# The opening of a fused attention and feed-forward kernel: half of k by a hardware queue, q in token quarters, v in three pieces

## The chip, the cores and the metric

The kernel runs on one core of a Trainium2 chip. A core has a matrix engine (TensorE, PE in the profile), a vector engine (VectorE, DVE), a scalar engine (ScalarE, ACT), a general engine (GpSimd, POOL), a queue engine for transfers (SyncE, SP) and 16 DMA engines that move data between HBM and the on-chip memory SBUF. Matrix products land in PSUM banks and must be copied out by DVE or ACT. Each engine works through its own instructions strictly in program order; they meet at semaphores. The metric is the device time of one execution in microseconds (us).

## The reference

```
k_proj = einsum('ks,bhsd->bhkd', E, k)      # E: [64, 1024]
v_proj = einsum('ks,bhsd->bhkd', F, v)
attn   = softmax(q @ k_proj^T / sqrt(64))   # over 64 projected keys
o      = attn @ v_proj                      # 8 batches, 8 heads, 1024 tokens, 64
x      = o, heads side by side              # [8192 tokens, 512]
g      = x @ w_gate                         # [512, 1536]
out    = (g * sigmoid(g) * (x @ w_val)) @ w_out
```

Everything comes in as float32 and is worked on in bfloat16 with float32 sums.

## The kernel before

**Tiling.** A batch is cut into two chunks of 512 tokens (`ch`); the feed-forward layer works chunk by chunk (`c` = 2 x batch + `ch`), each chunk in 12 tiles of 128 hidden columns (`f`). For each `f` there are four gate products into a bank of kind "g" and four value products into a bank of kind "v" (`f_mm`, L314, 512 columns each), a tanh on ACT (L334), two vector instructions on DVE (L341, L346), and later the products with `w_out` (L360). There are two "g" banks, so the gate products of `f` = 2 wait until DVE has read the gate of `f` = 0.

**Attention units.** `u_KV` (L137) projects k or v for a range of heads: eight accumulating products over the tokens, then for k one ACT copy (`ks`, L157), for v two ACT copies in batch 0 into the block-diagonal `BDV` (L162, L163). `u_KT` (L167) transposes the projected k on PE and copies it into `BD` by four DVE copies (L180, L181). A chunk's queries are handled in four units `u`: `g` is the half of the heads and `i` the half of the chunk's tokens (units 0 and 1 are heads 0 to 3, units 2 and 3 heads 4 to 7; units 0 and 2 are the first token half, 1 and 3 the second). For each unit: `u_T` four transposes and one copy to `qT`; `u_S` four score products and the exponential on ACT (`ee`, L231); `u_R` sum and reciprocal on DVE; `u_N` the normalising multiply (L258; POOL for units 0 and 1, DVE for units 2 and 3 of batch 0); `u_A` four transposes and one copy to `AT`. `u_PV2` (L294) multiplies two head pairs of one token half by `BDV`, and its copy gives half a chunk of `xT` (two of four pairs), the input of `f_mm`.

**The order is written out by hand.** After the opening (L427 to L521), a slot table runs the feed-forward of chunk `c` with the attention of later batches laid between. The opening runs batch 0's first chunk's attention as its data land. All loads of q, k, v and weights are issued by POOL, which casts float32 to bfloat16 on the way, in this order: k heads 0 to 3, k heads 4 to 7, q heads 0 to 3, q heads 4 to 7, v heads 0 to 3, v heads 4 to 7, then the weights of `f` = 0, 1, 2-3, 4-5, then q of the second chunk, and the rest. SP loads E and F as they are. Loads on POOL and the `u_N` multiplies of POOL share one order. `warm(n)` is n products of zeros that keep PE busy. `turn(0)` and `turn(1)` transpose E and F.

**The end of the opening** is: `u_KV` of v heads 4 to 7, `u_PV2` twice for the first token half, `u_A(0,1)` and `u_A(0,3)`, gate and value of `f` = 0 on the first token half, `u_PV2` twice for the second half, then `f` = 1 on the first half. The loop begins with `f` = 0 and 1 on the second half and then takes whole chunks from `f` = 2.

Of the kernel before, what the change touches and what calls it, by code (L numbers as in the profile page):

```python
# [12 lines left out]
BF16 = mybir.dt.bfloat16  # L13
FP32 = mybir.dt.float32

B = 8
H = 8
S = 1024
D = 64
KP = 64  # L20
DM = H * D
DFF = 1536
P = 128
NJ = S // P
# [4 lines left out]
CW = 512  # L29
# [5 lines left out]
def kernel(  # L35
# [19 lines left out]
    nc = tc.nc  # L55
# [4 lines left out]
    kv_pool = ctx.enter_context(tc.tile_pool(name="kv", bufs=2))  # L60
# [22 lines left out]
    kb, vb, qb, xT, hT = {}, {}, {}, {}, {}  # L83

    def load_k(b, h0=0, h1=H):
        if h0 == 0:
            kb[b] = kv_pool.tile([P, H, NJ, D], BF16, name="kb", tag="kb")
        nc.gpsimd.dma_start(  # L88
            out=kb[b][:, h0:h1].rearrange("p h j d -> p h (j d)"),
            in_=k[b, h0:h1].rearrange("h (p j) d -> p h (j d)", j=NJ),  # L90
        )

    def load_v(b, heads=(0, H)):
        t = kv_pool.tile([P, H, NJ, D], BF16, name="vb", tag="vb")
        vb[b] = t
        for h0, h1 in zip(heads, heads[1:]):
            nc.gpsimd.dma_start(
                out=t[:, h0:h1].rearrange("p h j d -> p h (j d)"),
                in_=v[b, h0:h1].rearrange("h (p j) d -> p h (j d)", j=NJ),
            )  # L100

    def load_q(b, ch, parts=1):
        t = q_pool.tile([P, H, 4, D], BF16, name="qb", tag="qb")
        qb[b, ch] = t
        n = H // parts
        for i in range(parts):
            nc.gpsimd.dma_start(  # L107
                out=t[:, i * n : (i + 1) * n].rearrange("p h j d -> p h (j d)"),
                in_=q[b, i * n : (i + 1) * n].rearrange("h (p c j) d -> p c h (j d)", c=2, j=4)[:, ch],
            )  # L110

    def load_w_gv(c0, c1, which=(0, 1)):
        cs = slice(c0 * P, c1 * P)
        for wsrc, wdst in [((moe_w_gate, wg), (moe_w_val, wv))[i] for i in which]:
            nc.gpsimd.dma_start(
                out=wdst[:, :, cs],
                in_=wsrc[:, cs].rearrange("(t p) c -> p t c", p=P),
            )
# [11 lines left out]
    def bank(where, shape, dt, name):  # L130
        pool, tag = banks[where]
        return pool.tile(shape, dt, name=name, tag=tag)

    def copy(eng, out, in_):
        (nc.scalar.copy if eng is nc.scalar else eng.tensor_copy)(out=out, in_=in_)  # L135
# [51 lines left out]
    def u_T(b, u, at="a", eng=nc.scalar):  # L187
        ch, w = divmod(u, 4)
        g, i = divmod(w, 2)
        ps = bank(at, [P, 4, P], BF16, "qTp")  # L190
        src = qb[b, ch]
        for n in range(4):
            nc.tensor.transpose(  # L193
                out=ps[:, n, :],
                in_=src[:, 4 * g + n, 2 * i : 2 * i + 2, :].rearrange("p j d -> p (j d)"),
                identity=ident_bf[:],
            )
        t = aw.tile([P, 4, P], BF16, name="qT", tag="qT", bufs=4)
        copy(eng, t[:], ps[:])
        qT[b, u] = t  # L200
# [38 lines left out]
    def u_R(b, u):  # L239
        e = ee[b, u]  # L240
        z = aw.tile([P, 4, 2], FP32, name="zz", tag="zz", bufs=3)
        nc.vector.reduce_sum(out=z[:], in_=e[:], axis=AX.X)  # L242
        r = aw.tile([P, 4, 2], FP32, name="rr", tag="rr", bufs=4)
        nc.vector.reciprocal(out=r[:], in_=z[:])  # L244
        rr[b, u] = r
# [48 lines left out]
    def u_PV2(b, ch, g, i, eng):  # L294
# [11 lines left out]
            )  # L306
        copy(eng, xT[b, ch][:, 2 * g : 2 * g + 2, 256 * i : 256 * (i + 1)], ps[:])


    gp = {}  # L310

# [112 lines left out]
            fn(*a)  # L424

    with tc.manual_schedule():
        load_k(0, 0, 4)  # L427
        ef = []
        for which, src in (("E", E), ("F", F)):
            raw = const.tile([KP, S], FP32, name=f"{which}raw")  # L430
            nc.sync.dma_start(out=raw[:], in_=src)
            ef.append(raw)
        zeros = const.tile([P, CW], BF16, name="zeros")
        nc.vector.memset(zeros[:], 0.0)
        make_identity(nc, ident_fp[:])
        make_identity(nc, ident_bf[:])
        for i in range(2):
            nc.vector.memset(BD[i][:], 0.0)
            nc.vector.memset(BDV[i][:], 0.0)

        def turn(which):
            for half in range(2):
                ps = bank("v", [P, 4, KP], FP32, "efp")
                for i in range(4):
                    j = 4 * half + i
                    nc.tensor.transpose(
                        out=ps[:, i, :],
                        in_=ef[which][:, bass.ds(j, P, step=NJ)],
                        identity=ident_fp[:KP, :KP],
                    )  # L450
                js = slice(4 * half, 4 * half + 4)
                copy((nc.scalar, nc.vector)[which], (ET, FT)[which][:, js, :], ps[:])

        def warm(n):

            ps = bank("v", [P, CW], FP32, "warm")
            for _ in range(n):
                nc.tensor.matmul(
                    out=ps[:], lhsT=zeros[:, 0:P], rhs=zeros[:],
                    start=True, stop=True,  # L460
                )


        load_k(0, 4, 8)
        load_q(0, 0, 2)
        load_v(0, (0, 4, 8))
        load_w_gv(0, 1)
        load_w_gv(1, 2)
        load_w_gv(2, 4)
        warm(8)  # L470
        turn(0)
        turn(1)
        warm(7)
        u_KV(0, "k", (0, 4), at="y")
        warm(2)
        u_KT(0, at="v", prs=(0, 2))
        warm(2)
        u_KV(0, "k", (4, 8), at="y")
        warm(2)
        u_KT(0, at="v", prs=(2, 4))  # L480
        u_T(0, 0, "a", nc.scalar)
        u_T(0, 1, "a", nc.vector)
        u_T(0, 2, "a", nc.scalar)
        u_S(0, 0, "g")
        u_T(0, 3, "v", nc.vector)
        u_S(0, 2, "g")
        u_S(0, 1, "a")
        u_S(0, 3, "a")
        u_R(0, 0)
        u_N(0, 0)  # L490
        u_R(0, 2)
        u_N(0, 2)
        load_w_gv(4, 6, (0,))
        u_KV(0, "v", (0, 4), at="y")
        warm(1)
        u_A(0, 0, nc.scalar)
        u_R(0, 1)
        u_N(0, 1)
        u_R(0, 3)
        u_N(0, 3)  # L500
        u_A(0, 2, nc.scalar)
        u_KV(0, "v", (4, 8), at="y")
        load_w_gv(4, 6, (1,))
        load_q(0, 1)
        load_w_gv(6, 8)
        load_w_gv(8, 10)
        load_w_gv(10, 12)
        load_wo(0)
        load_wo(1)
        load_k(1)  # L510
        warm(1)
        u_PV2(0, 0, 0, 0, nc.scalar)
        u_PV2(0, 0, 1, 0, nc.vector)
        u_A(0, 1, nc.scalar)
        u_A(0, 3, nc.vector)
        f_mm(0, 0, 0, 0)
        f_mm(0, 0, 1, 0)
        u_PV2(0, 0, 0, 1, nc.scalar)
        u_PV2(0, 0, 1, 1, nc.vector)
        f_mm(0, 1, 0, 0)  # L520
        f_mm(0, 1, 1, 0)  # L521

        for i, u in enumerate(range(4, 8)):
            put(12 + i, u_T, 0, u)
            put(14 + i, u_S, 0, u)
            put(15 + i, u_R, 0, u)
            put(15 + i, u_N, 0, u)
            put(19 + i, u_A, 0, u, nc.scalar)
        put(21, u_PV, 0, 1, 0)
        put(22, u_PV, 0, 1, 1)  # L530
        put(23, u_PV, 0, 1, 2)
        put(23, u_PV, 0, 1, 3)
        put(20, load_q, 1, 0)
        put(20, load_v, 1)
        put(20, load_q, 1, 1)
        for b in range(1, B):
            place(b)
        for b in range(2, B):
            s0 = 48 * (b - 1) - (12 if b == 2 else 24)
            put(s0, load_k, b)  # L540
            put(s0 + 2, load_v, b)
            put(s0 + 4, load_q, b, 0)
            put(s0 + 6, load_q, b, 1)

        for s in slots:
            slots[s].sort(key=lambda x: x[0] not in (load_k, load_v, load_q))


        ypart = defaultdict(list)
        for c in range(B * CH - 1):  # L550
            for n in range(NFT):
                f = n if c else 4 + (2 * n + 1) // 3
                ypart[(c + 1) * NFT + f].append((c, n))

        for t in range(NIT):
            c, f = divmod(t, NFT)
            i = 1 if t < 2 else None
            f_g(c, f, i)
            run_slot(2 * t)
            f_v(c, f, i)  # L560
            for a in ypart.pop(t, ()):
                f_y(*a)
            run_slot(2 * t + 1)
        for n in range(9):
            f_y(B * CH - 1, n)
        f_y_last(B * CH - 1, 3)
        assert not slots and not ypart
# [29 lines left out]
```

The softmax here doesn't subtract the row's maximum and nothing guards it: scores larger than these inputs give would overflow.

## Time and profile before

| | |
|---|---|
| median of 9 runs | 573.79 us (572.69 to 574.09) |
| the profiled execution | 573.77 us, of which 572.0 us lie between its first and last instruction |
| PE | 561.1 us busy, 98% |
| DVE, ACT, POOL | 337.0, 237.0, 108.0 us busy |
| granted PE clock | full, mean 1.000 |
| DMA | 61.34 MB written, mean 107 GB/s; 192 to 207 GB/s from 8 us to 32 us |
| first gate product of `f` = 0 | 22.17 us |
| first gate product of `f` = 2 | 26.48 us |

Bytes are counted where they are written. A casting load reads twice what it writes, so the 205 GB/s of the opening are 410 GB/s read. "To landing" is counted from the start of the issuing instruction. A line number can be that of a helper: L135 is the copy of all units.

### The profile page before, as it was taken

What the parts mean: (1) busy time and instruction counts of PE and PEld (TensorE: products, weight loads), DVE (VectorE), ACT (ScalarE), POOL (GpSimd) and SP (SyncE); (2) the same over time, 40 slices, a digit from 0 to 9 for tenths busy, and PEclk for the clock granted to TensorE, in tenths of its full rate; (3) what the DMA queues carried; (4) which work ended last, traced back from release to release, by engine and by line L of the source; (5) the groups of instructions that cost most, each with busy time, mean ns of one, the idle gap of its engine ahead of it and who ended that gap; (6) DMA issues with size and microseconds to landing.
All of it is one profiled execution on the core that took longest, in us unless ns stands there. A gap on an engine that the chain in (4) does not pass through costs nothing.

```text
span 572.0 us, 7867 instructions
## 1 busy us (share of the span) xinstructions
PE 561.1 (98%) x2910; PEld 268.5 (47%) x2967; DVE 337.0 (59%) x580; ACT 237.0 (41%) x416; POOL 108.0 (19%) x121
## 2 busy tenths in 40 slices
PE   8899999999999999999999999999999999999997
PEld 4654444444444444444444444444444444444444
DVE  2787566666466754766556665567546674554550
ACT  2665444354435434444335434354342543443232
POOL 6724121134002500124001330023200220000000
PEclk9999999999999999999999999999999999999999
DMA  9999993549901697038941399204990124100012
GB/s 170 195 201 205 201 152 75 92 69 192 203 34 46 113 190 150 18 75 129 190 105 38 63 176 198 60 20 92 190 180 36 45 49 74 38 37 26 30 39 92
DMA packets 105928, 61.34 MB, mean 107 GB/s; under 512 B 58017, under 2 KB 97697, under 8 KB 105889
## 3 DMA queue, kind: packets, MB, share of 16 engines
q0 software_dynamic: 42288, 29.89, 36.1%
q1 hardware_dynamic: 63312, 30.68, 25.2%
q8 instruction: 23, 0.38, 0.3%
q10 hardware_dynamic: 288, 0.26, 0.1%
q14 instruction: 17, 0.13, 0.1%
HBM read 60.29 MB, written 16.78 MB: 135 GB/s over the span
## 4 chain that ended last, share of the span: by engine, by line
PE 94%; DMA 2%; POOL 1%; ACT 1%; issue 1%; DVE 0%; POOLq 0%
PE yps L360 29%; PE vps L322 29%; PE gps L322 29%; PE kvp L147 3%; PE sc L227 2%; DMA vb<-in_v_dram 2%; PE pv L285 2%; PE aTp L274 0%; ACT xT L135 0%; PE qTp L193 0%; POOL kb L88 0%; PE kTp L172 0%; POOL qb L107 0%; ACT th L334 0%; PE pv L300 0%
## 5 line engine op out<-in xcount | busy, mean ns | idle before, releaser
L341 DVE SCALAR_TENSOR_TENSOR s<-th,gps 128x512 f32<-128x512 f32 x192 | 130.6, 680 | 137.9 <-ACT th L334 137.7
L322 PE MATMUL gps<-xT,wg 128*128 128x512 bf16 (+1 forms) x755 | 195.7, 377 | 1.2
L322 PE MATMUL vps<-xT,wv 128*128 128x512 bf16 (+1 forms) x761 | 195.9, 377 | 0.8
L360 PE MATMUL yps<-wo,hT 128*128 128x512 bf16 (+2 forms) x761 | 191.6, 376 | 0.8
L334 ACT ACTIVATE th<-gps 128x512 f32<-128x512 f32 x192 | 114.6, 597 | 162.6 <-PE gps L322 155.1
L346 DVE TENSOR_TENSOR hT<-s,vps 128x512 bf16<-128x512 f32 x192 | 132.0, 688 | 22.1 <-PE vps L322 1.5
L360 PEld LDWEIGHTS <-hT 128*128 128x128 bf16 x780 | 76.1, 98 | 89.9
L258 POOL TENSOR_TENSOR AAd<-ee,rr 128x512 bf16<-128x512 f32 x52 | 54.1, 1041 | 319.4 <-issue 168.4
L322 PEld LDWEIGHTS <-wv 128*128 128x128 bf16 x776 | 73.9, 98 | 82.9 <-issue 3.3
L322 PEld LDWEIGHTS <-wg 128*128 128x128 bf16 x776 | 74.0, 98 | 81.3 <-issue 0.6
L370 ACT ACTIVATE ysb<-yps 128x512 f32<-128x512 f32 (+1 forms) x65 | 38.4, 591 | 78.1 <-PE yps L360 74.4
L135 ACT CAST xT<-pv 128x512 bf16<-128x512 f32 x62 | 36.1, 585 | 51.3 <-PE pv L285 50.3
L242 DVE TENSOR_REDUCE zz<-ee 128x8 f32<-128x512 f32 x64 | 43.5, 679 | 17.9 <-ACT ee L231 17.9
L231 ACT ACTIVATE ee<-sc 128x512 f32<-128x512 f32 x64 | 37.9, 595 | 17.4 <-PE sc L227 17.4
L285 PE MATMUL pv<-AT,BDV 128*128 128x512 bf16 x60 | 22.6, 379 | 0.1
L227 PEld LDWEIGHTS <-qTd 128*128 128x128 bf16 x208 | 16.0, 98 | 12.3
L227 PE MATMUL sc<-BD,qTd 128*128 128x128 bf16 x208 | 20.1, 219 | 0.1
L135 DVE CAST BDV<-kvp 64x256 bf16<-64x256 f32 x14 | 6.0, 427 | 22.1 <-ACT ks L157 19.1
L258 POOL TENSOR_TENSOR AA<-ee,rr 128x512 bf16<-128x512 f32 x10 | 10.3, 1040 | 35.2 <-DVE rr L244 33.5
L244 DVE RECIPROCAL rr<-zz 128x8 f32<-128x8 f32 x64 | 13.0, 203 | 6.2
L147 PE MATMUL kvp<-vb,FT 128*64 128x512 bf16 (+1 forms) x72 | 15.5, 358 | 1.0 <-DMA vb<-in_v_dram 1.0
L147 PE MATMUL kvp<-kb,ET 128*64 128x512 bf16 (+1 forms) x72 | 15.5, 357 | 0.4 <-DMA kb<-in_k_dram 0.3
(49 smaller groups left out, 144.9 us busy)
## 6 DMA issues: line engine op xcount, KB each, us to landing
out_dram<-ysb SPq DMA_DIRECT2D x63, 256.0 KB, 2.3
qb<-in_q_dram POOLq DMA_DIRECT2D x15, 512.0 KB, 16.9
kb<-in_k_dram POOLq DMA_DIRECT2D x7, 1024.0 KB, 11.3
vb<-in_v_dram POOLq DMA_DIRECT2D x7, 1024.0 KB, 13.8
wo<-in_moe_w_out_dram POOLq DMA_DIRECT2D x2, 768.0 KB, 15.0
wg<-in_moe_w_gate_dram POOLq DMA_DIRECT2D x5, 256.0 KB, 10.4
wv<-in_moe_w_val_dram POOLq DMA_DIRECT2D x5, 256.0 KB, 10.4
kb<-in_k_dram POOLq DMA_DIRECT2D x2, 512.0 KB, 8.3
```

Of the source, the lines that this page charges most:

```text
L135: (nc.scalar.copy if eng is nc.scalar else eng.tensor_copy)(out=out, in_=in_)
L147: nc.tensor.matmul(out=t[lo : lo + 64, h0:h1].rearrange("p h d -> p (h d)"), lhsT=w[:, j, :], rhs=src[b][:, h0:h1, j, :], start=(j == 0), ...
L227: nc.tensor.matmul(out=ps[:, n, :], lhsT=t[:, n, :], rhs=BD[b % 2][:, 4 * g + n, :], start=True, stop=True)
L231: nc.scalar.activation(out=e[:].rearrange("p h j k -> p (h j k)"), in_=ps[:].rearrange("p a k -> p (a k)"), func=AF.Exp, scale=scale,)
L242: nc.vector.reduce_sum(out=z[:], in_=e[:], axis=AX.X)
L258: eng.tensor_tensor(out=a.rearrange("p j h k -> p h j k"), in0=ee.pop((b, u))[:], in1=rr.pop((b, u))[:].unsqueeze(3).to_broadcast([P, 4, 2 ...
L322: nc.tensor.matmul(out=ps[:, ts], lhsT=(wg, wv)[w][:, kt, f * P : (f + 1) * P], rhs=x[:, kt, ts], start=(kt == 0), stop=(kt == NKT - 1),)
L334: nc.scalar.activation(out=th[:], in_=ps[:], func=AF.Tanh, scale=0.5)
L341: nc.vector.scalar_tensor_tensor(out=s1[:], in0=th[:], scalar=1.0, in1=g[:], op0=ALU.add, op1=ALU.mult)
L346: nc.vector.tensor_tensor(out=hT[c][:, f, :], in0=s1[:], in1=ps[:], op=ALU.mult)
L360: nc.tensor.matmul(out=yy[c][:, cs], lhsT=hT[c][:, f, i * P : (i + 1) * P], rhs=wo[:, f, cs], start=(f == 0), stop=(f == NFT - 1),)
L370: nc.scalar.activation(out=ysb[:, cs], in_=yy[c][:, cs], func=AF.Copy, scale=0.5)
```

## The change

Heads 0 to 3 of batch 0's k are loaded as float32 by two transfers on ACT's own queue, into two buffers `kraw` that borrow space of tiles that are used later. DVE casts heads 0, 1, 2 and half of head 3, ACT the other half of head 3. POOL's first load is now k heads 4 to 7. The first chunk's q is loaded as its first token half for all heads (`js` 0 to 2), then v heads 0 to 3, then the second token half of q, then v heads 4-5 and v heads 6-7. The units follow: first token half first (units 0 and 2 before the first v, units 1 and 3 after it). `turn(1)` moves behind the first half of k, and its copies from DVE to ACT; there are fewer `warm` products. The last two head pairs of the first token half are multiplied one by one (`u_PV1`, new). `u_A(0,1)` and `u_A(0,3)` move behind the first `f_mm` of gate and value, and the second `u_PV2` pair behind the gate of `f` = 1. Weights of `f` = 2-3 are issued behind the first v projection, those of 4-5 (both matrices together) at the end. Nothing changes from the loop on.

```diff
-        if h0 == 0:
+        if b:
             kb[b] = kv_pool.tile([P, H, NJ, D], BF16, name="kb", tag="kb")
...
-    def load_q(b, ch, parts=1):
...
+    def load_q(b, ch, js=(0, 4)):
+        if js[0] == 0:
+            qb[b, ch] = q_pool.tile([P, H, 4, D], BF16, name="qb", tag="qb")
+        js = slice(*js)
+        nc.gpsimd.dma_start(
+            out=qb[b, ch][:, :, js, :].rearrange("p h j d -> p h (j d)"),
+            in_=q[b].rearrange("h (p c j) d -> p c h j d", c=2, j=4)[:, ch, :, js, :].rearrange(
+                "p h j d -> p h (j d)"
+            ),
+        )
...
+    def u_PV1(b, ch, pr, i, eng):
+
+        ps = ps_a.tile([P, CW // 2], FP32, name="pv", tag="pa")
+        nc.tensor.matmul(
+            out=ps[:].rearrange("p (j t) -> p j t", t=P),
+            lhsT=BDV[b % 2][:, pr, :],
+            rhs=AT[b, ch][:, 2 * i : 2 * i + 2, pr, :],
+            start=True,
+            stop=True,
+        )
+        copy(eng, xT[b, ch][:, pr, 256 * i : 256 * (i + 1)], ps[:])
...
-        load_k(0, 0, 4)
+        kb[0] = kv_pool.tile([P, H, NJ, D], BF16, name="kb", tag="kb")
+        kraw = [aw.tile([P, 2, NJ * D], FP32, name="kraw", tag=tag) for tag in ("qTd", "AAd")]
+        for i in range(2):
+            nc.scalar.dma_start(
+                out=kraw[i][:],
+                in_=k[0, 2 * i : 2 * i + 2].rearrange("h (p j) d -> p h (j d)", j=NJ),
+            )
...
+        load_k(0, 4, 8)
...
-                copy((nc.scalar, nc.vector)[which], (ET, FT)[which][:, js, :], ps[:])
+                copy(nc.scalar, (ET, FT)[which][:, js, :], ps[:])
...
-        load_k(0, 4, 8)
-        load_q(0, 0, 2)
-        load_v(0, (0, 4, 8))
-        load_w_gv(0, 1)
-        load_w_gv(1, 2)
-        load_w_gv(2, 4)
+        dve, act = nc.vector, nc.scalar
+        load_q(0, 0, (0, 2))
+        load_v(0, (0, 4))
+        load_q(0, 0, (2, 4))
+        load_v(0, (4, 6, 8))
+        for f in range(2):
+            load_w_gv(f, f + 1)
         warm(8)
-        turn(0)
-        turn(1)
-        warm(7)
+        turn(0, "v")
+        warm(4)
+        for h in range(4):
+            for n in range(2):
+                eng = act if (h, n) == (3, 1) else dve
+                ds = slice(256 * n, 256 * (n + 1)) if h == 3 else slice(0, 512)
+                if n == 0 or h == 3:
+                    copy(eng, kb[0][:, h].rearrange("p j d -> p (j d)")[:, ds], kraw[h // 2][:, h % 2, ds])
         u_KV(0, "k", (0, 4), at="y")
-        warm(2)
+        warm(1)
         u_KT(0, at="v", prs=(0, 2))
-        warm(2)
+        turn(1, "a")
+        warm(1)
         u_KV(0, "k", (4, 8), at="y")
         warm(2)
         u_KT(0, at="v", prs=(2, 4))
-        u_T(0, 0, "a", nc.scalar)
-        u_T(0, 1, "a", nc.vector)
-        u_T(0, 2, "a", nc.scalar)
+        u_T(0, 0, "a", act)
+        u_T(0, 2, "a", dve)
+        warm(1)
         u_S(0, 0, "g")
-        u_T(0, 3, "v", nc.vector)
         u_S(0, 2, "g")
-        u_S(0, 1, "a")
-        u_S(0, 3, "a")
+        warm(1)
         u_R(0, 0)
         u_N(0, 0)
         u_R(0, 2)
         u_N(0, 2)
-        load_w_gv(4, 6, (0,))
         u_KV(0, "v", (0, 4), at="y")
+        load_w_gv(2, 4)
         warm(1)
-        u_A(0, 0, nc.scalar)
+        u_T(0, 1, "a", act)
+        u_T(0, 3, "a", dve)
+        warm(2)
+        u_A(0, 0, act)
+        u_S(0, 1, "g")
+        u_A(0, 2, dve)
         u_R(0, 1)
         u_N(0, 1)
+        u_S(0, 3, "g")
         u_R(0, 3)
         u_N(0, 3)
-        u_A(0, 2, nc.scalar)
-        u_KV(0, "v", (4, 8), at="y")
-        load_w_gv(4, 6, (1,))
+        u_PV2(0, 0, 0, 0, act)
+        u_KV(0, "v", (4, 6), at="y")
+        warm(1)
+        u_PV1(0, 0, 2, 0, act)
+        u_KV(0, "v", (6, 8), at="y")
+        warm(1)
+        u_PV1(0, 0, 3, 0, act)
+        load_w_gv(4, 6)
         load_q(0, 1)
...
-        warm(1)
-        u_PV2(0, 0, 0, 0, nc.scalar)
-        u_PV2(0, 0, 1, 0, nc.vector)
-        u_A(0, 1, nc.scalar)
-        u_A(0, 3, nc.vector)
         f_mm(0, 0, 0, 0)
+        u_A(0, 1, act)
         f_mm(0, 0, 1, 0)
-        u_PV2(0, 0, 0, 1, nc.scalar)
-        u_PV2(0, 0, 1, 1, nc.vector)
+        u_A(0, 3, dve)
         f_mm(0, 1, 0, 0)
+        u_PV2(0, 0, 0, 1, act)
+        u_PV2(0, 0, 1, 1, dve)
         f_mm(0, 1, 1, 0)
```

More of the change, by code (lines that the diff above doesn't have):

```diff
@@ L93, in load_v @@
     def load_v(b, heads=(0, H)):
-        t = kv_pool.tile([P, H, NJ, D], BF16, name="vb", tag="vb")
-        vb[b] = t
+        if heads[0] == 0:
+            vb[b] = kv_pool.tile([P, H, NJ, D], BF16, name="vb", tag="vb")
+        t = vb[b]
         for h0, h1 in zip(heads, heads[1:]):
@@ L100, in load_v @@
             )
-    def load_q(b, ch, parts=1):
[L103 to L110, printed above, removed]
+    def load_q(b, ch, js=(0, 4)):
[8 more added lines that the diff above has]
+        )
     def load_w_gv(c0, c1, which=(0, 1)):
@@ L439, with turn @@
             nc.vector.memset(BDV[i][:], 0.0)
-        def turn(which):
+        def turn(which, at):
             for half in range(2):
-                ps = bank("v", [P, 4, KP], FP32, "efp")
+                ps = bank(at, [P, 4, KP], FP32, "efp")
                 for i in range(4):
@@ L492 @@
         u_N(0, 2)
-        load_w_gv(4, 6, (0,))
         u_KV(0, "v", (0, 4), at="y")
+        load_w_gv(2, 4)
         warm(1)
-        u_A(0, 0, nc.scalar)
+        u_T(0, 1, "a", act)
[4 more added lines that the diff above has]
+        u_A(0, 2, dve)
         u_R(0, 1)
         u_N(0, 1)
+        u_S(0, 3, "g")
         u_R(0, 3)
         u_N(0, 3)
-        u_A(0, 2, nc.scalar)
-        u_KV(0, "v", (4, 8), at="y")
-        load_w_gv(4, 6, (1,))
+        u_PV2(0, 0, 0, 0, act)
[6 more added lines that the diff above has]
+        load_w_gv(4, 6)
         load_q(0, 1)
-        load_w_gv(6, 8)
-        load_w_gv(8, 10)
-        load_w_gv(10, 12)
+        for f in (6, 8, 10):
+            load_w_gv(f, f + 2)
         load_wo(0)
```

## The prediction, made before the result was known

> **What bounds the kernel now.** First the page's chain of the work that ended last. PE has 94% of it, so almost every us in which PE's dense stream begins later or earlier is a us of the total.
>
> ```profile
> PE 94%; DMA 2%; POOL 1%; ACT 1%; issue 1%; DVE 0%; POOLq 0%
> ```
>
> The 2% of DMA is the opening. The same chain over the first 60 us:
>
> ```profile
> 6.20 13.41 DMA vb<-in_v_dram
> 19.61 0.04 issue
> 19.65 1.07 PE kvp L147 x8
> 20.73 0.02 issue
> 20.75 0.26 ACT BDV L135
> ...
> 21.34 0.39 PE pv L300 x2
> 21.73 0.60 PE aTp L274 x8
> 22.33 0.56 PE gps L322 x4
> ...
> 25.11 0.61 ACT th L334
> 25.72 0.02 issue
> 25.74 0.70 DVE s L341
> 26.44 0.04 issue
> 26.48 0.38 PE gps L322
> ```
>
> The last v lands at 19.61, its projection and copies follow, then the first gate. At 26.48 the gate of f = 2 begins, after the tanh and the DVE instruction that free its bank. From there on both kernels run the same instructions, so **I predict the shift of this one matmul, and that is the change of the time**.
>
> What feeds the chain is the DMA. The table by stage (last columns: share of the DMA engines, GB/s written):
>
> ```profile
> 2.50:3.00 0.50, 0.50 (x3) 0.23 (x2) 0.27 (x1) 0.00 (x0) 0.43 (x2) 1.00 0.88 319
> 3.50:4.00 0.50, 0.50 (x3) 0.15 (x1) 0.00 (x0) 0.00 (x0) 0.50 (x1) 1.00 0.72 197
> 4.50:5.00 0.50, 0.50 (x4) 0.28 (x3) 0.00 (x0) 0.00 (x0) 0.50 (x2) 1.00 0.98 156
> 8.50:9.00 0.50, 0.50 (x4) 0.13 (x2) 0.00 (x0) 0.00 (x0) 0.00 (x0) 1.00 1.22 203
> ```
>
> The queue view of the first 4.0 us shows 0.42 MB on SP's hardware queue and none on POOL's, whose first packets show by 4.5. So there is room from 2.3 to 6 us; from 7 us on the casting loads write 0.205 MB/us, that is read 0.41. Last, the timeline for ACT and DVE work:
>
> ```profile
> 14.58 0.40 PE L193 MATMUL qTp<-ident_bf,qb 128*128 128x128 bf16 x4 [0.41 <-DMA qb<-in_q_dram]
> 15.02 0.59 ACT L135 COPY qT<-qTp 128x512 bf16<-128x512 bf16 x1 [0.44 <-PE qTp L193]
> 15.50 2.17 ACT L231 ACTIVATE ee<-sc 128x512 f32<-128x512 f32 x4
> 18.18 0.54 ACT L135 CAST BDV<-kvp 64x128 bf16<-64x128 f32 x2 [0.51 <-PE kvp L147]
> ```
>
> From transposes to copy 0.44; four exponentials in 2.17, 0.54 each.
>
> **Part 1: the transfers.** Landings before: k 9.35 and 11.87, q 13.4 and 14.55, v 17.07 and 19.6, weights 20.3, 21.07, 21.8, 22.55. The second q half, call its landing L, comes after the same amount read as the first v half did: E and F 0.52, k 2.10, q 1.05, v 1.05, together 4.72 MB. So L is 17.07, corrected by two terms.
>
> *Two queues early.* By 4.4 E and F alone moved 0.49 MB; two rings at the full 0.41 MB/us would move 0.86 from 2.3 on; I take 0.70. Up to 8 us the old rate of 0.33 (4.5 to 6, hardware and POOL queue mixed) to 0.40 rises to 0.37 throughout, so 2.03 MB instead of 1.78 (0.52 plus twice 0.63): 0.25 MB at 0.41, and 0.2 more for the rings that no longer wait behind the first POOL load: 0.8 us gained. Bounds: 1.3 gained (0.86 MB, then 0.41); 0.75 lost, if all of E, F and k goes at the mixed 0.33 (ending at 10.8 instead of 10.05). I take 0.8, nearer the gain, because the share of 0.72 to 0.98 before 5 us says that the engines were short of work.
>
> [...]
>
> *Shorter rows.* q's halves are written in rows of 256 B instead of 512. The first weights have such rows: 128 KB every 0.75 us, against 512 KB of v every 2.53 (0.63 per 128 KB). Four times 0.12 is 0.48; by the rates (0.18 against 0.205 MB/us at 18 to 21) 0.35. I take 0.4.
>
> L = 17.07 - 0.8 + 0.4 = **16.7** (bounds 16.1 to 18.3). v 4-5 and v 6-7 follow 1.27 apart: 18.0 and 19.2; the last v lands only 0.4 earlier than before. The cut of v costs nothing by itself (same rows); POOL's issues (0.75 to 0.9 each) are covered while loads stay queued.
>
> **Part 2: from L to the gate, on ACT.** Nine ACT instructions stand in order between them. From L: transposes of unit 1 and copy 0.44 + 0.59, done 1.06. `u_A(0,0)` stands on PE behind unit 3's transposes and two warm products (0.22 each), so its copy runs 1.3 to 1.85 (0.55, the pitch of like copies at 18.75). Two exponentials 2.95. PV copy 3.5. Two BDV casts of 64x64, 0.22 each (on the line through 0.26 for 64x128 and 0.37 for 64x256): 3.95. PV of pair 2 0.35 to its copy, 0.37 for 128x256: 4.7. v 6-7 landed at L + 2.5, but its products are queued on PE behind that PV, which waits for the casts: 4.05 + eight at 0.055 + 0.2 = 4.7. Casts 5.2, PV 5.55, copy 5.9, **the fourth gate product L + 5.95 to 6.05** (22.75; before 22.73). So the shorter last v is paid for by the place of its work behind ACT: from its landing alone the gate would be at V + 2.0, L + 4.5.
>
> **Part 3: after the first gate.** `u_A(0,1)`, `u_A(0,3)` (0.22 each) were done before it and now are not. PE from the gate's end: 0.22, value 0.44, 0.22, gate of f = 1 0.44, two PV 0.44: 1.76; value of f = 1 to 2.2. DVE's `xT` cast (0.69) starts 0.2 after the PV, at 1.96, ends 2.65; then two products of the other gate half 2.9, tanh 3.1 to 3.7, DVE 4.42, f = 2 at 4.45. Before, from 22.73 to 26.48 was 3.75. **Cost 0.7.** Normalising of units 1 and 3 hides: exponential done L + 2.4, sum and reciprocal 0.9, POOL 1.04, L + 4.5; the DVE one L + 5.3, both needed after L + 6. If that cover went, each 0.1 late would be 0.1 lost.
>
> Sum: 16.7 + 6.05 + 4.45 = 27.2 against 26.48: **0.7 us later**.
>
> **Part 4: k by ACT's queue and the casts.** Two issues of 0.57 (the rows of E and F) on ACT before the table load (1.28): hidden, the first ACT copy came at 5.46. If the table load is first, the loads start 1.3 later. Until 4.4 ACT's ring gets half, 0.35 MB; then a third while F lasts, then half of 0.37: 1.05 MB are moved at 7.9, landed at about 8.4 (F's last 0.01 MB landed 1.7 after the rest; bounds 7.5 to 9.6). Then 1.5 DVE casts: no SBUF cast in this trace; between 0.42 (bf16 copy) and 0.69 (128x512 PSUM cast), taken 0.55: 0.8. First half of k at 9.2 (before 9.35). But now `turn(1)` (0.95) lies between the halves: second half 12.0 (its data at 11.1; before 11.89). Then ks, `u_KT`, `u_T`, BD copies: exponentials from 15.0, DVE sums to 17.35, unit 2's multiply (0.92) to 18.3, `qT` of unit 3 18.7, its exponential 19.7, the rest as in part 2: fourth gate 22.75. So this chain ends just with L's. Fewer warm products cost nothing: they ran in PE's waiting. POOL's weights 4-5 now stand behind unit 1's multiply (about 21 instead of 18.21), but f = 4 needs them at 30.5, and 7 to 10.4 us to landing suffice; those of f = 6-7 had 1.2 to 1.5 us to spare (landed 31.9 and 33.2).
>
> [...]
>
> **Rivals.**
> *A, as worked out:* 0.7 later; own range 0.4 earlier (L 16.1, the chain 0.5 shorter) to 1.1 later (L 17.1).
> *B, k is the late one:* each 0.1 that the raw k lands after 8.4 delays everything equally. For it: the ring is shared with POOL's, F's tail of 1.7, a table load ahead, and PE idle for 2 us before k (the first eight warm products took 0.45 each, later ones 0.24; at that pace the first half of k costs 0.9 more). At 9.4: 1.7 later. Against: queues idle before 4.4.
> *C, faster, v decides:* if L is early by more than the chain assumes and BDV is cast as v lands, the gate is at V + 2.0 and f = 2 at L + 8.95; with L 16.1 that is 25.05, 1.4 earlier. It decides when ACT is 1.5 shorter than summed; the 0.54 pitch speaks against.
> *D, weights:* the queue runs dry behind POOL's multiply and f = 6 waits: 1.5 later in all, from some 1.2 of dry queue on.
>
> **How the numbers follow.** The profiled execution is 573.77 (572.0 span, 1.77 around it), 0.02 below the median 573.79. 573.79 + 0.7 = 574.5. 0.2% is 1.15 us, about what a measurement of this kernel can tell from no change. Chances: A 0.52, nearly all within; B 0.26, slower; D 0.07, slower; C 0.15, faster. So faster 0.15, same 0.52, slower 0.33. Range: down to 1.1 earlier (572.7, leaving most of C out) and up to 2.2 later (576.0, B at 9.9).
>
> **What would show it.** Right: last v at 19.2 with its products starting over 1 us later, behind PV of pair 2; ACT without gaps from L to the gate; second q half at 16.7; gate of f = 2 at 27.2; then the old spacing. Wrong: first half of k after 9.5 (B); v's products starting as it lands and the gate before 21.5 (C); a wait on wg or wv after 30 us (D).

## The result, and the profile after

The changed kernel takes 577.33 us (median of 10 runs, 575.47 to 578.58), the kernel before 573.94 (31 runs). The ratio is 1.0053, 95% interval 1.0044 to 1.0062: **slower by 0.53%, 3.0 us** (3.4 in the medians), where 0.7 us had been forecast. The profiled execution is one of 577.54 us with a span of 575.8.

The marker that the prediction chose, the first gate product of f = 2, stands at 30.38 us instead of 26.48. That is 3.90 later, against 3.8 in the span: all of the loss arises in the opening, as it was argued, and behind it the two agree to 0.1.

On the page of the changed kernel the chain of the work that ended last has less DMA in it than before (2% there), and more ACT:

```profile
PE 95%; ACT 2%; DMA 1%; issue 1%; DVE 0%; POOL 0%; ACTq 0%; POOLq 0%
```

The same chain over the opening (start, duration, what):

```profile
1.25 7.03 DMA kraw<-in_k_dram
...
9.17 1.87 PE kvp L149 x8
11.04 0.54 PE warm L480
11.57 0.22 PE kTp L174 x2
11.79 0.92 PE efp L468 x8
12.71 0.54 PE warm L480
13.26 1.85 PE kvp L149 x8
15.10 0.54 PE warm L480
...
17.86 0.61 ACT ee L233
...
23.94 0.58 PE kvp L149 x8
24.54 0.21 ACT BDV L137
24.76 0.22 ACT BDV L137
...
25.34 0.38 ACT xT L137
...
30.38 0.38 PE gps L336
```

Before, the chain ran through v's landing. Now it goes through the raw k (landed at 8.3) and then through PE's own work on k, and later through the exponentials and ACT; v's landing is nowhere in it. Two lines are wrong beside those of before: each half of k's projection takes 1.85 to 1.87, where the same eight products took 1.03. PE's timeline before, and then after, shows from when on:

```profile
4.72 1.09 PE L446 MATMUL efp<-ident_fp,Eraw 64*128 64x64 f32 x8
...
7.57 1.67 PE L458 MATMUL warm<-zeros 128*128 128x512 bf16 x7
9.35 1.03 PE L147 MATMUL kvp<-kb,ET 128*64 128x256 bf16 x8
...
11.89 1.03 PE L147 MATMUL kvp<-kb,ET 128*64 128x256 bf16 x8 [0.27 <-DMA kb<-in_k_dram]
```

```profile
1.19 3.60 PE L480 MATMUL warm<-zeros 128*128 128x512 bf16 x8 [1.19 <-DVE zeros L456]
6.02 1.11 PE L468 MATMUL efp<-ident_fp,Eraw 64*128 64x64 f32 x8 [1.23 <-DMA Eraw<-in_E_dram]
7.15 1.86 PE L480 MATMUL warm<-zeros 128*128 128x512 bf16 x4
9.17 1.87 PE L149 MATMUL kvp<-kb,ET 128*64 128x256 bf16 x8 [0.15 <-DVE kb L137]
...
13.19 1.92 PE L149 MATMUL kvp<-kb,ET 128*64 128x256 bf16 x8
```

Eight warm products in 3.60 us is the slow pace, 0.43 each (the last one's end is modelled later). Before, E followed at 4.72, F at 6.43, and the seven warm products at 7.57 went at half of that, in 1.67. Now E lands only at 6.0: the raw k's first packets come at 2.0 us, and E's at 3.4 instead of 2.3. PE idles from 4.8 to 6.0, and the products behind it still go at 0.43. PE stays at the slow pace until 16.5 us.

The table by stage (PE, PEld, DVE, ACT, POOL busy, granted clock, DMA share, GB/s) shows the gain that was sought, and a granted clock that does not go with the pace:

```profile
2.50:3.00 0.50, 0.50 (x3) 0.22 (x2) 0.27 (x1) 0.50 (x1) 0.43 (x3) 1.00 1.07 401
3.50:4.00 0.50, 0.50 (x3) 0.15 (x1) 0.00 (x0) 0.00 (x0) 0.50 (x1) 1.00 0.97 369
4.50:5.00 0.50, 0.29 (x1) 0.00 (x0) 0.47 (x1) 0.00 (x0) 0.50 (x2) 1.00 1.09 205
14.00:15.00 1.00, 1.00 (x6) 0.54 (x4) 0.00 (x0) 0.00 (x0) 0.00 (x0) 1.00 1.83 185
```

From 2.5 to 3 us 401 GB/s move instead of 319. From 14 to 15 us PE is busy all the time, the granted clock is given as 1.00, and yet each product takes twice its time. That 1.00 is no reading. The clock's record in this trace begins only at 16.54 us, and the view counts the time ahead of it as full clock. From 16.54 on the record says full, and the pace agrees: q's transposes start up to 0.11 apart until 16.5, and some 0.06 apart from 16.6. In the kernel before, the record begins, at full clock, at 5.40, so its mean of 1.000 leaves out the first 5 us.

### The profile page after: what moved, and what is told of

The parts are those of the page before. It is cut to its first block, busy times and chain, and to the rows that moved or that the text cites. A ratio compares the mean times of both kernels' runs of the same rounds, so it can differ in the third digit from the quotient of the medians.

```text
span 575.8 us, 7894 instructions
## 1 busy us (share of the span) xinstructions
PE 564.9 (98%) x2918; PEld 269.6 (47%) x2975; DVE 337.8 (59%) x582; ACT 238.5 (41%) x422; POOL 108.6 (19%) x121
## 4 chain that ended last, share of the span: by engine, by line
PE 95%; ACT 2%; DMA 1%; issue 1%; DVE 0%; POOL 0%; ACTq 0%; POOLq 0%
PE yps L374 29%; PE vps L336 28%; PE gps L336 28%; PE kvp L149 3%; PE sc L229 3%; PE pv L287 2%; DMA kraw<-in_k_dram 1%; ACT xT L137 0%; PE aTp L276 0%; PE qTp L195 0%; PE kTp L174 0%; PE warm L480 0%; ACT ee L233 0%; ACT AT L137 0%; ACT th L348 0%
## 5 line engine op out<-in xcount | busy, mean ns | idle before, releaser
L137 ACT CAST xT<-pv 128x512 bf16<-128x512 f32 (+1 forms) x64 | 36.9, 578 | 51.8 <-PE pv L287 50.3
L149 PE MATMUL kvp<-kb,ET 128*64 128x512 bf16 (+1 forms) x72 | 17.2, 390 | 0.2 <-DVE kb L137 0.2
L149 PE MATMUL kvp<-vb,FT 128*64 128x512 bf16 (+2 forms) x80 | 15.7, 339 | 0.0
```

Of the source, the lines that this page charges most:

```text
L149: nc.tensor.matmul(out=t[lo : lo + 64, h0:h1].rearrange("p h d -> p (h d)"), lhsT=w[:, j, :], rhs=src[b][:, h0:h1, j, :], start=(j == 0), ...
```

## The experiments

Three theories were set against each other. **P**: PE's slow pace on the k chain costs the time. **Q**: the new order behind the second q half, on ACT and PE, costs it, and the pace is hidden. **D**: the hardware queue holds up POOL's loads. The ratios are to the kernel before, run beside each.

### More warm products

```diff
-        warm(8)
+        warm(12)
         turn(0, "v")
-        warm(4)
+        warm(6)
```

> The changed kernel with 12 warm products ahead of E's transposes instead of 8 and 6 behind them instead of 4. Theory P (PE stays at its slow pace, 0.43 us per warm product, up to 16 us because it idles from 4.8 to 6.0, and the projection of k stands on the path): the warm products behind E go at 0.22, each half of k takes 1.0 instead of 1.9, the gate of f = 2 starts near 27.4 instead of 30.4, the time is 574.3 to 575.0. Rival Q (the new order behind the second half of q, on ACT and PE, costs the time; the pace is hidden): no change, 577. Rival D (the hardware queue holds up POOL's loads): no change, 577.

Measured: 574.80 us, ratio 1.0026 (1.0016 to 1.0035). PE's timeline of this run:

```profile
1.19 5.30 PE L480 MATMUL warm<-zeros 128*128 128x512 bf16 x12 [1.19 <-DVE zeros L456]
6.42 1.09 PE L468 MATMUL efp<-ident_fp,Eraw 64*128 64x64 f32 x8
7.58 1.46 PE L480 MATMUL warm<-zeros 128*128 128x512 bf16 x6
8.96 1.06 PE L149 MATMUL kvp<-kb,ET 128*64 128x256 bf16 x8
...
11.87 1.06 PE L149 MATMUL kvp<-kb,ET 128*64 128x256 bf16 x8
```

PE has six products more to do and ends earlier. From the start of k's first half to the first exponential it takes 6.12 (8.96 to 15.08) instead of 8.69 (9.17 to 17.86), so 2.57 less; the gate of f = 2 moves from 30.38 to 27.59. The profiled executions differ by 2.78 (577.54 and 574.76), the medians by 2.5, the ratios by 0.27% (1.5 us). The ratio's share is smaller because three of the changed kernel's executions took only 575.5. The clock's record begins, at full clock, at 6.98 in this run and at 16.54 in the changed kernel. P holds, Q and D alone do not.

### All of k by POOL

The two raw loads, their buffers and the casts are taken out again, and POOL issues both halves of k first; everything else stays as changed.

```diff
-        kraw = [aw.tile([P, 2, NJ * D], FP32, name="kraw", tag=tag) for tag in ("qTd", "AAd")]
...
+        load_k(0, 0, 4)
```

> The changed kernel with heads 0 to 3 of k loaded by POOL as before, without raw buffers and casts. E lands at 4.4 again. P: PE does not idle before E's transposes, gets to its fast pace by 8 us or soon after, the k halves start at 9.4 and 11.9; all other loads land 0.8 later than in the changed kernel, so the gate of f = 2 is at 28.0 and the time 575.2 (576 if PE stays slow with 4 warm products). Q: 577 or more, as the order is kept. D: 574 to 575, as POOL's loads start at once; its landings would then be earlier than in the changed kernel.

Measured: 577.64 us, ratio 1.0071 (1.0057 to 1.0085), far above the 575.2 that P gave, and above its 576 too. The timeline says why:

```profile
5.65 1.02 PE L475 MATMUL warm<-zeros 128*128 128x512 bf16 x4
...
9.11 1.86 PE L149 MATMUL kvp<-kb,ET 128*64 128x256 bf16 x8 [2.43 <-DMA kb<-in_k_dram]
```

In this run the table by stage shows the pace as well, in the granted clock (third column from the end):

```profile
7.00:8.00 1.00, 0.00 (x0) 0.00 (x0) 0.00 (x0) 0.00 (x0) 1.00 (x3) 0.85 1.02 152
14.00:15.00 1.00, 1.00 (x6) 0.54 (x5) 0.00 (x0) 0.00 (x0) 0.08 (x1) 0.50 1.61 183
```

Here PE did reach its fast pace, 0.22 per product at 5.65; the clock's record begins at 4.29. Then it waited 2.43 us for k, and was slow again: by the record the clock fell to half at 7.71 and was full again at 17.95. My expectation had PE fast once and for all; the four products behind E were too few to bridge the wait. D falls: with the hardware queue gone, the time is no better, and POOL's loads end later, not earlier.

This run also prices the transfers apart. POOL's queue had written all of k, q and v (2.62 MB) at 17.84 us before, at 18.28 here; in the changed kernel it had written its part (2.10 MB) at 17.72. So the shorter q rows, with the new order and the cut of v, cost 0.44, and the hardware queue brings 0.56. Between the two runs with PE kept fast (below, and 12 and 6 products) the same end lies 0.9 apart, at about 18.4 and 17.5, so these prices are good to some 0.3.

### All of k by POOL, PE kept busy

The same with 14 warm products behind E's transposes instead of 4.

> All of k by POOL, as in the second experiment, and 14 instead of 4 warm products behind E's transposes, so that PE does not idle for 2.4 us ahead of k. P: PE keeps 0.22 per warm product up to k at 9.1 and both halves of k take 1.0; time 574.8 to 575.3, not 577.6. What the hardware queue is worth in time is then the difference to the run with 12 and 6 warm products (574.8): 0 to 0.5. If the hardware queue itself costs or saves more: outside of that.

Measured: 575.32 us, ratio 1.0028 (1.0017 to 1.0039). Both halves of k take 1.03 to 1.06. It is 2.3 below the run with 4 products, which shows the price of the pace in an order without any hardware queue. Against the run with 12 and 6 products (574.80) the hardware queue is worth 0.5 in the medians; by the ratios, 0.0002 apart, nothing that these runs can tell.

### The idle time kept, products added behind it

```diff
         turn(0, "v")
-        warm(4)
+        warm(6)
```

> The changed kernel with 6 warm products behind E's transposes instead of 4, but only 8 ahead of them, so that PE idles from 4.8 to 5.9 as in the changed kernel. If that idle time is what leaves PE slow: the 6 go at 0.43 (2.6 us instead of 1.3), both halves of k take 1.9, and since the 6 now end at 9.6, after the casts of k, the time is 577.3 to 578. If the number of products behind E's transposes is what counts: 0.22 each, 574.8.

Measured: 576.11 us (574.77 to 576.73), ratio 1.0035 (1.0023 to 1.0048), between the two answers:

```profile
7.06 2.39 PE L480 MATMUL warm<-zeros 128*128 128x512 bf16 x6
9.38 1.75 PE L149 MATMUL kvp<-kb,ET 128*64 128x256 bf16 x8
...
12.98 1.06 PE L149 MATMUL kvp<-kb,ET 128*64 128x256 bf16 x8
```

```profile
8.00:9.00 1.00, 1.00 (x4) 0.27 (x2) 0.73 (x2) 0.41 (x1) 1.00 (x2) 0.50 1.23 206
11.00:12.00 1.00, 0.86 (x8) 0.51 (x7) 0.14 (x1) 0.36 (x1) 0.64 (x1) 1.00 1.30 206
```

The first half of k is slow, the second is not. The clock's record of this trace begins, at full clock, at 4.02, ahead of the idle time; it falls to half at 7.43, when the six products have begun (the first two start 0.22 to 0.26 apart, the later ones 0.43), and is full again from 10.84. In the changed kernel's trace the clock had not come up at all by then, though the two programs are the same up to these products. So when the clock comes up differs between executions of like instructions, and this trace cannot tell what the six products did and what that did. The idle time kept and six products instead of four: 576.11 against 577.33 is all that is shown, and the intervals of their ratios overlap a little.

### The kernel before, made slow

```diff
-        warm(8)
         turn(0)
         turn(1)
-        warm(7)
```

> The kernel before without its first 8 and its next 7 warm products. P: PE is slow through both halves of k as in the changed kernel (1.9 each), but here v's landing at 19.6 covers it: turn(1) stands ahead of k and the k chain has some 3 us to spare, so the time rises by at most 1 us (PE may be slow for the first gates, each at twice 0.11 per 256 columns). If the slow pace alone cost 3 us whatever the order: 577.

Measured: 574.64 us, ratio 1.0015 (1.0004 to 1.0026), 0.9 us. PE's k work is as slow as in the changed kernel (timeline), yet more than half of it is hidden (chain, last two lines):

```profile
9.15 1.86 PE L147 MATMUL kvp<-kb,ET 128*64 128x256 bf16 x8 [1.72 <-DMA kb<-in_k_dram]
...
13.09 1.87 PE L147 MATMUL kvp<-kb,ET 128*64 128x256 bf16 x8
```

```profile
20.85 1.00 PE kvp L147 x8
...
27.61 0.38 PE gps L322
```

The last v projection starts 1.2 later than before (19.65), now behind the k chain, and the gate moves by 1.1 only. The old order hides some 60% of what the new one pays (1.1 against the 2.8 between 30.38 and 27.59), since `turn(1)` stands ahead of k, and in the kernel before v's landing is the bound and leaves the k chain time to spare. The clock's record begins at 14.78 here, as against 16.54; both halves of k were slow in either. So it is the new order that puts PE's pace on the path, and the pace that makes it dear.

### F's transposes moved

```diff
-        turn(1, "a")
         warm(1)
         u_KV(0, "k", (4, 8), at="y")
...
+        turn(1, "a")
         u_KV(0, "v", (0, 4), at="y")
```

> The changed kernel with the transposes of F moved from between the two halves of k to just ahead of the first v projection. P with the k chain on the path: the second half of k, and all behind it, starts 1.1 earlier (0.9 to 1.1 of slow transposes), the time falls by 0.9 to 1.1, to about 576.4. Q and D: the k chain is not the bound, no change, 577.3.

Measured: 575.54 us, ratio 1.0044 (1.0032 to 1.0057). The time falls, as P has it, by more in the medians (1.8) than the 1.1 expected. In the profiled execution (576.69) the second half of k took 1.44 and was partly fast (the clock's record begins at 13.27), so this run does not separate the move from the pace. The same move with PE kept fast:

> 12 and 6 warm products, and the transposes of F moved behind the scores, ahead of the first v projection. With PE at its fast pace they cost 0.9 to 1.1 between the halves of k. If the k chain still sets the end there (unit 1's transposes ran at 16.9, after the first v projection, while the second q half had landed by about 16.6): earlier by what the chain has over L, 0.3 to 0.8, time 574.0 to 574.5. If the landing of the second q half already sets it: no change, 574.8.

Measured: 574.86 us, ratio 1.0019 (1.0010 to 1.0027), against 574.80 and 1.0026: no difference. I had overlooked that the transposes, in their new place, still stand ahead of unit 1's on PE; those started at 16.70 instead of 16.88. The run says nothing on L.

### The end of the opening, piece by piece

All of these have the 12 and 6 warm products. First, the order of before for the transposes of units 1 and 3 and for the second PV pair:

```diff
+        u_A(0, 1, act)
+        u_A(0, 3, dve)
         f_mm(0, 0, 0, 0)
-        u_A(0, 1, act)
         f_mm(0, 0, 1, 0)
-        u_A(0, 3, dve)
-        f_mm(0, 1, 0, 0)
         u_PV2(0, 0, 0, 1, act)
         u_PV2(0, 0, 1, 1, dve)
+        f_mm(0, 1, 0, 0)
```

> 12 and 6 warm products, and the end of the opening in the order of before: unit 1's and unit 3's transposes ahead of the first gate, the second PV pair behind gate and value of f = 0. Part 3 of the prediction charges the moved order 0.7: then the gate of f = 2 follows the last xT copy by 3.8 instead of 4.6, and the time is 574.2 or a little more, since the transposes now delay the first gate by what they overhang PE's wait. If the moved order costs nothing: 574.8.

Measured: 574.35 us, ratio 1.0005 (0.9996 to 1.0013): 0.45 less in the medians, and the gate of f = 2 at 26.76 instead of 27.59, 0.83 earlier. Of the 0.83, 0.22 were there ahead of the moved pieces (the PV product of pair 3 at 22.01 instead of 22.23), so the moved order costs 0.61 in the traces, close to part 3's 0.7. Second, v ahead of the PV products:

```diff
-        u_PV2(0, 0, 0, 0, act)
         u_KV(0, "v", (4, 6), at="y")
+        u_PV2(0, 0, 0, 0, act)
         warm(1)
-        u_PV1(0, 0, 2, 0, act)
         u_KV(0, "v", (6, 8), at="y")
         warm(1)
+        u_PV1(0, 0, 2, 0, act)
```

> 12 and 6 warm products, and v heads 4-5 projected ahead of the first PV pair, v heads 6-7 ahead of the PV of pair 2, which then runs beside pair 3's. Part 2 of the prediction: the last v's work stands behind ACT's casts and the PV of pair 2, though v has landed. If so the last xT copy ends at 22.2 instead of 22.9 and the time falls by 0.6 to 0.8, to 574.1. If the landing of the last v sets it: no change, 574.8.

Measured: 574.17 us, ratio 1.0005 (0.9996 to 1.0014), 0.63 less, as part 2 has it (in the profiled executions the gate of f = 2 is 0.34 earlier, with the first half of k started 0.3 later). Its chain is still ACT, from the exponentials to the last copy, but for the products of v 6-7:

```profile
19.27 0.99 ACT ee L233 x2
...
20.29 0.21 ACT BDV L137
20.51 0.22 ACT BDV L137
...
20.77 0.62 PE kvp L149 x8
21.41 0.21 ACT BDV L137
21.63 0.21 ACT BDV L137
...
21.86 0.73 ACT xT L137 x2
```

The products of v 6-7 start as the casts of 4-5 end. To see whether they wait for them through the bank that the pieces share, they got a bank of their own (`u_KV(0, "v", (6, 8), at="v")`):

> As the run with v ahead of the PV products, but v heads 6-7 are projected into a PSUM bank of their own. There their first product started at 20.77, just as the casts of heads 4-5 ended at 20.73, though the data had landed by about 19.3: if the pieces wait for each other's casts because they share a bank, the products now start by 19.6 and the time falls by up to 0.5, to 573.7; ACT's order of casts and copies may keep part of it. If they waited for the data or for PE's order, they start at 20.7 again, 574.2.

Measured: 574.33 us, ratio 1.0010 (1.0001 to 1.0019): no gain. The products started at 20.56, 0.15 ahead of the casts' end, but the casts of 6-7 had to follow ACT's casts and copy of the first pairs, and began at 21.33, where they began at 21.41 in the run before. ACT, at work without a gap in the chain from 18.68 to 22.51, is what sets this stretch.

### Versions meant to beat both

All three changes, F's transposes late, pairs 2 and 3 in one product pair:

> A version meant to beat both: 11 and 5 warm products, F's transposes late, v ahead of the PV products, pairs 2 and 3 in one PV product pair and copy, units 1 and 3 transposed ahead of the first gate with both copies on DVE, the rest in the order of before. If the three terms add (0.5, 0.7, 0.7): gate of f = 2 near 25.9, 572.8 to 573.2. If they share one bound, the landing of the last v at about 19.2: 573.3 to 573.8, as before.

Measured: 573.88 us, ratio 1.0000 (0.9991 to 1.0010), the gate of f = 2 at 26.26. Then v 6-7 in its own bank, both casts ahead of the PV copies, unit 3's transposes behind the first gate:

> The version of all three terms with v heads 6-7 in a bank of their own, the two casts of 4-5 and 6-7 ahead of the first PV copies on ACT, and unit 3's transposes behind the first gate, since DVE's multiply for it ended at 21.8 and held the gate back there. If the shared bank and that multiply were its bounds: gate of f = 2 near 25.6 (26.26 there, 26.48 before), time 573.0 to 573.3. If ACT's order is the bound: 573.8.

Measured: 573.88 us, ratio 1.0002 (0.9993 to 1.0011). In its profiled execution (573.15) the gate is at 25.96, and its bound is now POOL's multiply for unit 1:

```profile
20.20 1.05 POOL AA L260
...
21.29 0.40 PE aTp L276 x4
21.69 0.44 PE gps L336 x4
...
25.96 1.02 PE gps L336 x4
```

The profiled execution's 0.5 us does not show in the timed runs. Nothing tried beats the kernel before.

## Why the prediction was wrong

The forecast was 574.5 us, 572.7 to 576.0, with no clear change as the likeliest; the kernel took 577.33. **The step that failed is in part 4: "Fewer warm products cost nothing: they ran in PE's waiting."** The warm products were what kept PE's pace up through that waiting: with 12 and 6 of them both halves of k took 1.06, with 8 and 4 1.87 and 1.92. With too few of them, and with E's transposes 1.3 us later, both halves of k, and the products of zeros between and behind them, ran at half pace (F's transposes, 1.11 against 1.07, hardly slower), at a clock that the trace records as full only from 16.54 us instead of 5.40: 2.57 us from the start of k to the first exponential, 2.5 in the medians. Rival B named the cause, PE's idle time and the 0.45 and 0.24 per product, but charged it with 0.9 for one half of k and only as a possibility. The rows for the full price were there: all of the k chain's PE work stood in a sum that had no slack.

With PE kept busy the forecast's own sum can be read off (run with 12 and 6 products), and it was too small by a little: the gate of f = 2 is 1.11 later than before, and the ratio 1.0026 is 1.5 us (0.9 to 2.0), against 0.7.

- *Raw k at 8.4:* it landed at 8.3. Casts of 0.55: DVE took 0.41 to 0.62, the first half of k started at 9.17 (9.2 forecast).
- *Two queues, 0.8:* 0.56, and 0.9 between the two runs with PE kept fast. *Shorter rows, 0.4:* 0.44, with the new order in it. The hardware queues did not only fill idle time: POOL's first packets came at 6.2 us instead of 4.1. POOL's last v had left the queue at 17.72; with the 1.8 from there to landing that the v of before shows (17.84 and 19.6), an estimate, it landed at 19.5 (19.2 forecast). That the engines were short of work before 4.5 is the likely reason for the 0.56 (a share of 0.72 from 3.5 to 4 us became 0.97). The time shows 0.5 of it in the medians of the two runs with PE kept fast, and nothing by their ratios.
- *Part 2, 6.05 from L to the gate's end:* from unit 1's transposes at 16.88 to the gate's end at 23.25, 6.37. Eleven ACT instructions stand there, not nine, though the sum has them all. ACT is not without gaps: in the run with 12 and 6 products it stands still for 0.42, 0.38, 0.19 and 0.38 us, each time until a PE product is done. But the last v's work waits behind it, as forecast; moving v ahead gave the 0.6.
- *Part 3, 4.45 from there, 0.7 of it for the moved order:* 4.34, and 0.45 (medians) to 0.61 (traces).
- *Rival C, v decides:* not in any run, not even where ACT's order was changed. *Rival D:* the queue did run dry behind POOL's multiply, 1 GB/s from 21 to 22 us in the changed kernel, but no wait on weights appears in the chain.
- *POOL's issues, covered while loads stay queued:* the second q issue, beside DVE's first casts of the raw k, took 1.08 against 0.91 of the q issue ahead of it; at most 0.2, with loads queued.

## What to carry to other kernels

Products that only keep PE busy are part of the timing (six of them were worth 2.5 us in the changed kernel): before any are dropped, or a transfer that they bridge is moved, look at how long PE's like products take on either side of the gap, and at where the clock's record begins: a granted clock of 1.00 can mean that nothing is recorded yet (up to 16.54 us in the changed kernel). An opening bound by transfers can forgive slow compute: the one before let 1.1 us of PE's slow pace through to the gate of f = 2. The order that feeds compute earlier and lets less wait for the last transfer let 2.8 through, and put the place of v's work on ACT (0.6 in the time) on the path as well. And a transfer that ends earlier need not be worth that: POOL's loads ended 0.9 earlier in one of the two runs with PE kept fast, and their ratios lie 0.0002 apart.

## What the runs showed of the hardware

- **A granted clock of 1.00 can stand beside half the pace.** 512 columns take 0.43 us or 0.22, and in the changed kernel the view gives 1.00 for both. The clock's record begins with full clock, in the changed kernel just where the pace doubles: at 5.40 us before, 16.54 in the changed kernel, 6.98 with 12 and 6 warm products, 13.27 with F's transposes moved, 14.78 in the kernel before made slow. What lies ahead is counted as full. Where the clock falls after it has once come up, the rows do show 0.50: from 7.71 to 17.95 with all of k by POOL, 1.2 us after PE's last product, and from 7.43 to 10.84 with the idle time kept, amid products.
- The recorded stretches at half clock last 10.24 us and 3.41, a third of it. In the changed kernel PE was busy 0.98 to 1.00 of each us from 6 to 9, 0.85 from 9 to 10, and all the time from 10 to 15 us, and slow until 16.5. What brings the clock up was not shown; of the work in that stretch k's products, with 64 stationary columns, took 1.87 and 1.92 us and the fp32 transposes of 64 rows 1.11 twice.
- The changed kernel's executions lie at 575.5 and at 577 to 578.6. That this is the time at which the fast pace returns is likely, not shown, since one execution was profiled. The mean clocks of the others point to it. A mean of 0.997 stands for 3.4 us at half clock (which take 1.7 us from a span of 574), 0.991 for 10, as in the two profiled executions with those stretches (0.997 and 0.991): two of the three executions at 575.5 have 0.997 and none of the others has, while 576.99 has 0.994, and 577.72 and 578.58 have 0.991. The rest read 1.00, which says nothing.
